# Retention into an ELU feed-forward layer on one core: an order written by hand replaced by steps that a planner lists, with FFN blocks of 256 tokens

## The chip, the cores and the metric

One NeuronCore of a Trainium2 chip runs the whole program in one launch. TensorE (PE in the profile, PEld for its weight loads) does the matrix products, VectorE (DVE) and ScalarE (ACT) the work that reads PSUM, GpSimd (POOL) works on SBUF only, and SyncE (SP) issues DMAs. DMAs issued by SP go through a hardware queue (q1 in the profile), those issued by GpSimd through a software queue (q0). The metric is the device time of the program in microseconds, as the median of its runs.

## The reference, cut to what matters

```python
# q, k, v: float32 (8, 8, 576, 64): batch, heads, sequence, head size
scores = (1 / sqrt(64)) * q @ k^T
gamma  = 1 - 2 ** (-5 - head)                       # one decay per head
D      = gamma ** (i - j) where i >= j, else 0
ret    = (scores * D) @ v
x      = ret laid out as (8 * 576 = 4608 tokens, 512)
h      = x @ w_in                                   # w_in (512, 2048)
g      = where(h > 0, h, exp(min(h, 0)) - 1)        # ELU
out    = g @ w_out                                  # w_out (2048, 512), out (4608, 512) float32
```

All inputs are float32. The decay factors into a power of gamma on q and one on k, so each kernel scales q and k while casting them to bf16 and needs only a 0/1 mask on the scores.

## The kernel before, in words

**Retention.** A batch of 576 positions is cut into five units: four main units (sequence half T of 256 positions, group w of four heads) and one tail of 64 positions with all eight heads. That makes 40 units. A unit is loaded by three DMAs of SP (`load`, L180; tails L174), scaled and cast (`cast`, L191: four 128x256 products for q and k, on POOL or DVE; L217 for v), and its q and k are transposed: the first nine units on PE through the identity (`turn_pe`, L241, with copies out of PSUM, L242), the others by a DMA transpose of SP (`turn`, L230). `stretch(u)` is one visit of PE to retention: it does the products with the carried state (`inter`) and with v (`values`) of unit u-1, the scores and the new state of unit u. Between them DVE masks the scores (L292, tails L286), adds up the state (L381, L383, L388) and POOL spreads it into block-diagonal form (L372). ACT copies the finished retention to `xt` in bf16 (L345, tails L334).

**FFN.** Tokens are worked in nine groups of 512. `ffn1(g, ft)` makes 128 rows of the hidden layer by four matmuls of 512 columns into one PSUM bank `ph`; ACT takes the exponential (`e`, L467), DVE subtracts one (`em`, L471) or ACT takes the ReLU in place (L469), and DVE joins both (`g`, L476 or L478). `ffn2(g, it, fts)` adds up 128 tokens of the output in the bank `pm` by sixteen matmuls of 512 columns; ACT copies it out (L488) and the store goes from POOL's queue (L491), for the last group from SP's. Group 1 is worked in two parts, of 320 and 192 tokens.

**Weights.** `load_w` (L151) loads w_in and w_out as 32 float32 tiles of 256 KB from SP, `cast_w` (L156) casts each to bf16, 31 of them on POOL and one on ACT.

**Order.** Every instruction is issued in an order written by hand (`pin` keeps program order on each engine). The loads of units 0 to 3 come first on SP, then the 32 weight tiles, then the loads of units 4 to 11. The retention of batch 0's main units is the start; then group 0's FFN; then group 1's with the stretches of the next units spread by hand between; and from group 2 on `run` spreads the stretches evenly between alternating FFN1 and FFN2 calls. A stretch is followed by the loads five units ahead, the casts three ahead and the transpose two ahead (`step`).

PSUM has eight banks: three for `ph` (also for PE transposes), one for `pm`, two for the scores, two for `x`. Almost all PE instructions are recorded at the helper's line L66.

Of the kernel before, what the change touches and what calls it, by code (L numbers as in the profile page):

```python
# [13 lines left out]
ALU = mybir.AluOpType  # L14


@with_exitstack
def kernel(
# [9 lines left out]
    nc = tc.nc  # L28
# [4 lines left out]
    NTOK = B * S  # L33
    P = 128
# [6 lines left out]
    TG = 512  # L41
    NTG = NTOK // TG
    MID = S // 2
    NS = B * NU
# [4 lines left out]
    raw = ctx.enter_context(tc.tile_pool(name="raw", bufs=10))  # L49
    nat = ctx.enter_context(tc.tile_pool(name="nat", bufs=4))  # L50
    tpool = ctx.enter_context(tc.tile_pool(name="tpool", bufs=4))
    ppool = ctx.enter_context(tc.tile_pool(name="ppool", bufs=2))
    rpool = ctx.enter_context(tc.tile_pool(name="rpool", bufs=4))
    xpool = ctx.enter_context(tc.tile_pool(name="xpool", bufs=3))
    gpool = ctx.enter_context(tc.tile_pool(name="gpool", bufs=2 * NFT + 2))
    epool = ctx.enter_context(tc.tile_pool(name="epool", bufs=4))
    opool = ctx.enter_context(tc.tile_pool(name="opool", bufs=4))

    ps_h = ctx.enter_context(tc.tile_pool(name="ps_h", bufs=3, space=PSUM))
    ps_m = ctx.enter_context(tc.tile_pool(name="ps_m", bufs=1, space=PSUM))  # L60
    ps_s = ctx.enter_context(tc.tile_pool(name="ps_s", bufs=1, space=PSUM))
    ps_x = ctx.enter_context(tc.tile_pool(name="ps_x", bufs=1, space=PSUM))

    pin = tc.keep_in_program_order
    def mm(*a, **kw):
        pin(nc.tensor.matmul(*a, **kw))  # L66
# [3 lines left out]


    ident = const.tile([P, P], BF16, name="ident")
    make_identity(nc, ident)
    zero = const.tile([P, 512], BF16, name="zero")
    nc.vector.memset(zero, 0.0)
# [33 lines left out]

    mask = const.tile([P, 2, 2, C], BF16, name="mask")  # L110
    nc.vector.memset(mask, 1.0)
    for c in range(2):
        for ek in range(2):
            for eq in range(2):
# [3 lines left out]
    mask_t = const.tile([ST, ST], BF16, name="mask_t")  # L118
    nc.vector.memset(mask_t, 1.0)
    nc.gpsimd.affine_select(out=mask_t, in_=mask_t, compare_op=ALU.is_ge, fill=0.0, base=0, pattern=[[1, ST]],  # L120
                            channel_multiplier=-1)


    s_mid = [const.tile([P, 2, P], BF16, name=f"s_mid{w}") for w in range(2)]
    s_end = [[const.tile([P, 2, P], BF16, name=f"s_end{w}{t}") for t in range(2)] for w in range(2)]
# [9 lines left out]
    engines = {"v": nc.vector.tensor_copy, "s": nc.scalar.copy, "p": nc.gpsimd.tensor_copy}  # L135
    staged = {}

    def weights(k):
        for i in (2 * k, 2 * k + 1):
            n, j = divmod(i, KJ)  # L140
            if n < KJ:
                c = slice(n * 512, (n + 1) * 512)
                yield i % 2, moe_w_in[j * P : (j + 1) * P, c], w_in_sb[:, j, c]
            else:
                f = i - KJ * KJ
                yield i % 2, moe_w_out[f * P : (f + 1) * P, :], w_out_sb[:, f, :]

    def load_w(k):
        staged[k] = raw.tile([P, 2, 4, 2, D], FP32, name="rqk", tag="rqk").rearrange("p i h e d -> p i (h e d)")
        for h, src, dst in weights(k):  # L150
            pin(nc.sync.dma_start(staged[k][:, h], src))  # L151

    def cast_w(k, eng="pp"):
        for h, src, dst in weights(k):
            if eng[h] != " ":
                pin(engines[eng[h]](dst, staged[k][:, h]))  # L156


    rawt, natt, trt, ptt, score_ps, total = {}, {}, {}, {}, {}, {}
    xps, begun = [None, None], set()  # L160

    def unit(u):
        b, r = divmod(u, NU)
        return b, r // 2, r % 2, r == FT

    def load(u, last=False):
        if u >= NS:
            return
        b, T, w, tail = unit(u)
        if tail:  # L170
            rqk = raw.tile([P, H, D], FP32, name="rqt", tag="rqt", bufs=2)
            rv = raw.tile([ST, H, D], FP32, name="rvt", tag="rvt", bufs=2)
            for dst, src in ((rqk[:ST], q), (rqk[ST:], k), (rv, v)):
                pin(nc.sync.dma_start(dst, src[b, :, FT * P :, :].rearrange("h p d -> p h d")))  # L174
        else:
            rqk = raw.tile([P, 2, 4, 2, D], FP32, name="rqk", tag="rqk")
            rv = raw.tile([P, 4, 2, D], FP32, name="rv", tag="rv", bufs=7)
            parts = [(rqk[:, 0], q), (rqk[:, 1], k), (rv, v)]
            for dst, src in parts[2:] + parts[:2] if last else parts:
                pin(nc.sync.dma_start(  # L180
                    dst.rearrange("p h e d -> p h (e d)"),
                    src[b, 4 * w : 4 * w + 4, 2 * P * T : 2 * P * (T + 1), :].rearrange("h (p e) d -> p h (e d)", e=2),
                ))
        rawt[u] = rqk, rv

    def cast_q(u, eng, i=0, es=(0, 1)):
        b, T, w, tail = unit(u)
        x = rawt[u][0][:, i].rearrange("p h e d -> p e h d")
        g = (gq, gk)[i][:, 2 * T : 2 * T + 2, 4 * w : 4 * w + 4].unsqueeze(3).to_broadcast([P, 2, 4, D])
        for e in es:  # L190
            pin(eng.tensor_tensor(natt[u][0][:, i, e], x[:, e], g[:, e], ALU.mult))  # L191

    def cast(u, q="p", v="p"):
        if u >= NS:
            return
        b, T, w, tail = unit(u)
        rqk, rv = rawt[u]
        if tail:
            qkn = nat.tile([P, H, D], BF16, name="qkt", tag="qkt", bufs=2)
            vn = nat.tile([ST, H, D], BF16, name="vt", tag="vt", bufs=2)  # L200
            g = gq[:, FT].unsqueeze(2).to_broadcast([P, H, D])
            for hs in (slice(0, H // 2), slice(H // 2, H)):
                pin(nc.gpsimd.tensor_tensor(qkn[:, hs], rqk[:, hs], g[:, hs], ALU.mult))
            pin(nc.gpsimd.tensor_copy(vn, rv))
        else:
            qkn = nat.tile([P, 2, 2, 4, D], BF16, name="qkn", tag="qkn")
            vn = nat.tile([P, 4, 2, D], BF16, name="vn", tag="vn", bufs=5)
            natt[u] = qkn, vn
            if q:
                cast_q(u, nc.vector if q == "v" else nc.gpsimd)  # L210
                cast_q(u, nc.gpsimd, 1)
            if v:
                cast_v(u, v)
        natt[u] = qkn, vn

    def cast_v(u, eng):
        pin(engines[eng](natt[u][1], rawt[u][1]))  # L217

    def turn_tile(u):
        n = 4 if unit(u)[3] else 8  # L220
        trt[u] = tpool.tile([P, n, P], BF16, name="qkT", tag=f"qkT{n}")
        return n

    def flat(u):
        return natt[u][0].rearrange("p h d -> p (h d)" if unit(u)[3] else "p i e h d -> p (i e h d)")

    def turn(u):
        if u < NS:
            turn_tile(u)
            pin(nc.sync.dma_start_transpose(trt[u], flat(u)))  # L230

    def turn_pe(u, eng="vs", between=0):
        n = turn_tile(u)
        for i in range(2):
            if i and between:
                warm(between)
            if i * 4 < n:
                p = ps_h.tile([P, 4, P], BF16, name="ptr", tag="ph")
                for j in range(4):
                    lo = (i * 4 + j) * P  # L240
                    pin(nc.tensor.transpose(p[:, j], flat(u)[:, lo : lo + P], ident))  # L241
                pin(engines[eng[i]](trt[u][:, i * 4 : i * 4 + 4], p))  # L242

    def queries(u, rows, hl, c):

        return trt[u].rearrange("p (i h) n -> p i h n", h=2)[rows, 0:2, hl, c * C : (c + 1) * C]
# [3 lines left out]

    def new_x():
        for c in range(2):
            xps[c] = ps_x.tile([P, 512], FP32, name="x", tag=f"x{c}")
        begun.clear()

    def acc_x(c, half, out, lhsT, rhs, to=None):

        first = not ({half} if half < 2 else {0, 1}) & {h for cc, h in begun if cc == (c, id(to))}
        begun.update(((c, id(to)), h) for h in ((half,) if half < 2 else (0, 1)))
        mm(out, lhsT, rhs, start=first, stop=True, skip_group_check=True)  # L260

    def scores(u):
        b, T, w, tail = unit(u)
        sc = ps_s.tile([P, 2, 512], FP32, name="sc", tag="sc")
        if tail:
            for hp in range(HP):
                for i in range(2):
                    r = slice(i * D, (i + 1) * D)
                    mm(sc[:ST, i, hp * ST : (hp + 1) * ST], trt[u][r, hp, ST:], trt[u][r, hp, :ST], start=True, stop=True)
        else:  # L270
            for hl in range(2):
                for ek in range(2):
                    for i in range(2):
                        r = slice(i * D, (i + 1) * D)
# [422 lines left out]
```

## Time and profile before

| | |
|---|---|
| time, median of 3 runs | 336.96 us (336.87 to 337.36) |
| span of the profiled execution | 333.9 us, 3.1 us under the median |
| PE busy | 303.7 us (91%) |
| DVE, ACT, POOL busy | 208.1, 178.8, 180.7 us (62%, 54%, 54%) |
| read and written in HBM | 36.70 and 9.44 MB |
| chain that ended last | PE 76%, POOL 9%, DVE 4%, DMA 3%, ACT 3% |

The profile is of one execution, so sums made from its rows are compared with its span, 333.9 us, and the 3.1 us around it are added to compare with a median. PE's busy time counts each matmul to its modelled end, so an isolated one counts for more than the pitch of a stream; a few matmul records are missing. In rows of the timeline a start time, a length and a count are given for instructions merged into one row.

### The profile page before, as it was taken

How to read it: one execution, taken by the hardware profiler on the slowest of the kernel's cores; microseconds unless marked ns; L12 is line 12 of the kernel's file. 1: busy time of each engine (PE TensorE's matmuls, PEld its weight loads, DVE VectorE, ACT ScalarE, POOL GpSimd, SP SyncE). 2: the span in 40 equal slices, each digit the busy share in tenths (PEclk: the TensorE clock that was granted, in tenths of full speed). 3: DMA queues.
4: the chain of work that ended last, by engine and by line, in shares of the span. 5: the costliest groups of instructions: out<-in, count | busy, mean ns of one | idle time of the engine just before them, and what ended most of it. 6: DMA issues, size and time to landing. Idle time of an engine off the chain costs nothing.

```text
span 333.9 us, 7841 instructions
## 1 busy us (share of the span) xinstructions
PE 303.7 (91%) x3049; PEld 154.4 (46%) x3092; DVE 208.1 (62%) x378; ACT 178.8 (54%) x364; POOL 180.7 (54%) x316
## 2 busy tenths in 40 slices
PE   7789985767679999999999999999999999999995
PEld 2443442444455554444545445444544544444342
DVE  3868626487747997666758666866677654454400
ACT  3666523555436766555565656555565556546411
POOL 5899564478979887442675666676574110000100
PEclk9999999999979999999999999999999999999999
DMA  7999999505999999854469957795421100000021
GB/s 213 312 339 375 287 320 274 153 2 145 222 267 216 254 244 219 176 159 143 110 127 207 243 123 174 181 232 112 96 63 49 64 33 31 33 31 32 33 94 63
DMA packets 100293, 53.86 MB, mean 161 GB/s; under 512 B 44448, under 2 KB 93600, under 8 KB 100256
## 3 DMA queue, kind: packets, MB, share of 16 engines
q1 hardware_dynamic: 97696, 44.97, 56.5%
q0 software_dynamic: 2560, 8.39, 8.4%
q8 instruction: 24, 0.39, 0.5%
q14 instruction: 13, 0.11, 0.1%
HBM read 36.70 MB, written 9.44 MB: 138 GB/s over the span
## 4 chain that ended last, share of the span: by engine, by line
PE 76%; POOL 9%; DVE 4%; DMA 3%; ACT 3%; issue 2%; SPq 0%; POOLq 0%; ACTq 0%; DVEq 0%
PE pm L66 35%; PE ph L66 32%; PE x L66 5%; PE sc L66 3%; POOL qkn L191 3%; POOL w_in_sb L156 3%; DMA qkT<-qkn 2%; DMA rqk<-in_q_dram 2%; DVE pt L292 1%; DVE g L478 1%; ACT ot L488 1%; DVE em L471 1%; POOL s_mid_147 L372 1%; ACT xt L345 1%; ACT ph L469 1%
## 5 line engine op out<-in xcount | busy, mean ns | idle before, releaser
L66 PE MATMUL ph<-xt,w_in_sb 128*128 128x512 bf16 (+2 forms) x611 | 145.7, 358 | 6.6 <-DVE g L478 3.7
L66 PE MATMUL pm<-w_out_sb,g 128*128 128x512 bf16 x564 | 144.1, 380 | 3.2 <-ACT ot L488 1.7
L467 ACT ACTIVATE e<-ph 128x512 f32<-128x512 f32 (+2 forms) x152 | 87.3, 575 | 90.0 <-PE ph L66 78.8
L66 PEld LDWEIGHTS <-w_in_sb 128*128 128x128 bf16 x640 | 59.3, 98 | 66.2 <-issue 8.0
L66 PEld LDWEIGHTS <-g 128*128 128x128 bf16 x576 | 55.7, 98 | 70.1 <-issue 7.9
L476 DVE SCALAR_TENSOR_TENSOR g<-e,ph 128x512 bf16<-128x512 f32 (+2 forms) x80 | 50.3, 633 | 48.1 <-ACT ph L469 45.4
L471 DVE TENSOR_SCALAR em<-e 128x512 bf16<-128x512 f32 (+2 forms) x76 | 43.2, 569 | 31.4 <-ACT e L467 31.4
L491 POOL DMA_DIRECT2D out_dram<-ot x32 | 18.4, 576 | 77.4 <-ACT ot L488 77.4
L478 DVE SCALAR_TENSOR_TENSOR g<-ph,em 128x512 bf16<-128x512 f32 (+2 forms) x80 | 50.7, 638 | 3.7 <-DVE em L471 0.5
L469 ACT ACTIVATE ph<-ph 128x512 f32<-128x512 f32 (+2 forms) x76 | 43.3, 570 | 0.0
L292 DVE TENSOR_TENSOR pt<-sc,mask 128x1024 bf16<-128x1024 f32 x31 | 37.8, 1218 | 7.2 <-PE sc L66 7.2
L191 POOL TENSOR_TENSOR qkn<-rqk,gk 128x256 bf16<-128x256 f32 x64 | 38.5, 621 | 3.5 <-DMA rqk<-in_k_dram 3.5
L345 ACT CAST xt<-x 128x256 bf16<-128x256 f32 (+1 forms) x70 | 23.7, 419 | 26.3 <-PE x L66 26.2
L488 ACT COPY ot<-pm 128x512 f32<-128x512 f32 x36 | 21.1, 589 | 20.1 <-PE pm L66 20.1
L191 POOL TENSOR_TENSOR qkn<-rqk,gq 128x256 bf16<-128x256 f32 x52 | 31.5, 625 | 0.1
L372 POOL TENSOR_TENSOR s_mid_147<-mid,diag 128x256 bf16<-128x256 f32 x16 | 9.9, 618 | 26.8 <-DVE mid L383 14.2
L372 POOL TENSOR_TENSOR s_mid_146<-mid,diag 128x256 bf16<-128x256 f32 x16 | 9.7, 606 | 26.2 <-DVE mid L383 20.0
L66 PE MATMUL sc<-qkT 64*64 64x128 bf16 (+1 forms) x576 | 16.1, 222 | 3.2 <-DMA qkT<-qkn 2.8
L217 POOL CAST vn<-rv 128x512 bf16<-128x512 f32 x28 | 18.8, 671 | 0.0
L66 PEld LDWEIGHTS <-qkT 64*64 64x64 bf16 x576 | 10.0, 107 | 8.8 <-DMA qkT<-qkn 3.1
L66 PE MATMUL x<-pt,vn 64*64 64x128 bf16 x496 | 13.1, 221 | 0.0
L241 PE MATMUL ptr<-ident,qkn 128*128 128x128 bf16 x64 | 7.3, 227 | 5.7 <-POOL qkn L191 2.3
(79 smaller groups left out, 184.0 us busy)
## 6 DMA issues: line engine op xcount, KB each, us to landing
rqk<-in_q_dram SPq DMA_DIRECT2D x32, 256.0 KB, 4.5
rqk<-in_k_dram SPq DMA_DIRECT2D x32, 256.0 KB, 5.0
rv<-in_v_dram SPq DMA_DIRECT2D x32, 256.0 KB, 5.3
out_dram<-ot POOLq DMA_DIRECT2D x32, 256.0 KB, 3.8
rqk<-in_moe_w_in_dram SPq DMA_DIRECT2D x16, 256.0 KB, 5.7
rqk<-in_moe_w_out_dram SPq DMA_DIRECT2D x16, 256.0 KB, 5.5
rqt<-in_q_dram SPq DMA_DIRECT2D x8, 128.0 KB, 4.2
rqt<-in_k_dram SPq DMA_DIRECT2D x8, 128.0 KB, 4.1
```

What stands on the lines that cost most here:

```text
L66: pin(nc.tensor.matmul(*a, **kw))
L191: pin(eng.tensor_tensor(natt[u][0][:, i, e], x[:, e], g[:, e], ALU.mult))
L217: pin(engines[eng](natt[u][1], rawt[u][1]))
L292: pin(nc.vector.tensor_tensor(pt.rearrange("p i h n -> p (i h) n"), sc.rearrange("p i (h n) -> p (i h) n", h=2), mask.rearrange("p k e r - ...
L345: pin(engines[eng[c]](dst, src[:, :, :, a // 2 : (a + n) // 2]))
L372: pin(eng.tensor_tensor(dst.rearrange("p h (j d) -> p h j d", j=2), src.unsqueeze(2).to_broadcast([P, 2, 2, D]), diag.unsqueeze(1).unsquee ...
L467: pin(nc.scalar.activation(e[:, :m], ph[:, :m], AF.Exp))
L469: pin(nc.scalar.activation(ph[:, :m], ph[:, :m], AF.Relu))
L471: pin(nc.vector.tensor_scalar_add(em[:, :m], e[:, :m], -1.0))
L476: pin(nc.vector.scalar_tensor_tensor(dst, e[:, c], -1.0, ph[:, c], ALU.add, ALU.min))
L478: pin(nc.vector.scalar_tensor_tensor(dst, ph[:, c], 0.0, em[:, c], ALU.max, ALU.min))
L488: pin(nc.scalar.copy(ot, pm))
```

## The change

The program is no longer issued in the order in which it is written. Each step (a load, a cast, a transpose, a stretch, an FFN piece, a store) is added to a list with the engines that may do it, a cost on each, what it depends on, a rank, and the buffer slots that it takes. A planner in the kernel then goes through time: it takes of the steps that are ready the one that can start first, of those that start within 0.05 us on the same engine the one of lowest rank, and gives it the engine on which it would end first. It does so eight times, with the transfers' times taken from the round before, keeps the order with the earliest end, and issues the program in that order. Beside this:

- FFN blocks have 256 tokens: two per batch (`seq` 0 to 15), and two blocks "A" and "B" of four tails each. A PSUM bank holds two 128-row pieces of the hidden layer side by side.
- A block needs two main units. Batch by batch the units are 0 to 3, 4 to 7, then the tails of both batches as one item, and so on: 36 items.
- Weights are cast by the DMA itself: eight transfers from POOL's queue, each reading 1 MB, each listed after a given step of the first units.
- The middle step of the ELU may go to ACT, DVE or POOL, the copies out of PSUM to ACT or DVE, the casts of q and k to POOL or DVE.
- All single `ph`, `pm`, transpose and early state banks share four PSUM slots "f"; scores have one slot of two banks, `x` one of two.
- Items 0 to 7 are transposed on PE, the others by DMA.

```diff
+HOP = {"PE": 0.24, "DVE": 0.08, "ACT": 0.08, "POOL": 0.1}
+LANES = 8
...
+            picks = list(best.values())
+            first = min(picks, key=lambda c: (c[1], c[2]))
+            same = [c for c in picks if c[3] == first[3] and c[1] <= first[1] + 0.05]
+            _, s, _, eng, pay, op = min(same, key=lambda c: (c[2], c[1]))
...
+def W_GATE(items, n):
+    return [items[2].cq[1, 1], items[3].cq[1, 1], items[3].bm, items[3].be][n]
+def WO_GATE(items, n):
+    return items[4].cq[1, 1] if n < 2 else items[5].cq[1, 1]
+LEAD = 64
+SLOTS = {
+    "f": 4, "sc": 1, "x": 1,
+    "rqk": 8, "rv": 8, "qkn": 5, "vn": 6, "qkT": 5, "pt": 3,
+    "rqt": 4, "rvt": 2, "qkt": 4, "vt": 2, "qkTt": 4, "ptt": 2,
+    "xt": 5, "g": 20, "e": 4, "em": 4, "ot": 4, "mid": 4, "end": 4, "s_mid": 4, "s_end": 8,
+}
...
-    def load_w(k):
-        staged[k] = raw.tile([P, 2, 4, 2, D], FP32, name="rqk", tag="rqk").rearrange("p i h e d -> p i (h e d)")
-        for h, src, dst in weights(k):
-            pin(nc.sync.dma_start(staged[k][:, h], src))
-    def cast_w(k, eng="pp"):
-        for h, src, dst in weights(k):
-            if eng[h] != " ":
-                pin(engines[eng[h]](dst, staged[k][:, h]))
...
+    seq = list(range(2 * B))
+    seq = [*seq[:B], "A", *seq[B:], "B"]
...
+    for it in items:
+        it.rank = it.n * 4 - 64 if it.early else place[it.blk] * 16 - LEAD + 6 * (it.half if it.tail else it.w)
...
+    def load_w_in(n0, n1, after):
+        c = slice(n0 * 512, n1 * 512)
+        def emit(op):
+            pin(nc.gpsimd.dma_start(w_in_sb[:, :, c], moe_w_in[:, c].rearrange("(j p) n -> p j n", p=P)))
+        op = add(f"wi{n0}", {"POOL": 1.1}, [], emit, -1000, dma=2.8 * (n1 - n0), after=after)
+    def load_w_out(n, after):
+        def emit(op):
+            pin(nc.gpsimd.dma_start(w_out_sb[:, 4 * n : 4 * n + 4],
+                                    moe_w_out[n * 512 : (n + 1) * 512, :].rearrange("(f p) n -> p f n", p=P)))
+        w_out_ld[n] = add(f"wo{n}", {"POOL": 1.1}, [], emit, -1000, dma=2.8, after=after)
...
+    def ffn1(blk, p):
...
+        rank = i * 16 + 2 * p
...
+            for f in range(2):
+                ft = 2 * p + f
+                for j in range(KJ):
+                    mm(ph[:, f * TB : (f + 1) * TB], w_in_sb[:, j, ft * P : (ft + 1) * P], xt[:, j],
+                       start=(j == 0), stop=(j == KJ - 1))
...
+        f1 = add(f"F1_{blk}_{p}", {"PE": 0.873}, [*xdone[blk], w_in_ld[p // 2]], emit, rank,
+                 take=[T("f", hkey, [P, 512], FP32)], use=[("xt", blk)], after=chain.get(1))
...
+        md = add(f"md_{blk}_{p}", {"ACT": 0.55, "DVE": 0.5, "POOL": (0.75, 0.1)}, [ex], emit_m, rank,
...
+    def ffn2(blk, it, c, per, rank):
...
+            for ft in range(c * per, (c + 1) * per):
+                g = tiles["g", blk, ft // 2].rearrange("p (f n) -> p f n", f=2)
+                mm(pm, g[:, ft % 2, it * P : (it + 1) * P], w_out_sb[:, ft], start=(ft == 0), stop=(ft == NFT - 1))
...
+    for n in range(4):
+        load_w_in(n, n + 1, W_GATE(items, n))
...
+    for n in range(4):
+        load_w_out(n, WO_GATE(items, n))
+    for i, blk in enumerate(seq):
+        for p in range(NP):
+            ffn1(blk, p)
+        if i == 0:
+            for c in range(8):
+                for it in range(2):
+                    ffn2(blk, it, c, 2, (i + 1) * 16 + 1 + 2 * c)
+        else:
+            for it in range(2):
+                for c in range(4):
+                    ffn2(blk, it, c, 4, (i + 1) * 16 + 8 * it + 2 * c + 1)
+    order = plan.run({"PE": 1.3, "DVE": 2.2, "ACT": 3.0, "POOL": 4.4, "SP": 0.8})
...
+        if op.eng == "PE":
+            if op.name.startswith("iv"):
+                for _ in range(int((op.start - last - 0.3) / 0.25)):
+                    mm(tiles[op.take[0][1]][:, 0], zero[:, :P], zero, start=True, stop=True)
```

## The prediction

> **What bounds the kernel now.** I read the page first (TensorE, "PE", is busy 91% of the span and holds 76% of the chain that ended last), then the busy time by stretch, to see where the other 9% lies.
>
> ```profile
> core 0: us, PE busy (x) PEld busy (x) DVE busy (x) ACT busy (x) POOL busy (x), PEclk, DMA share, GB/s
> 20.00:30.00 10.00, 8.90 (x38) 3.61 (x38) 7.98 (x14) 7.11 (x14) 10.00 (x18) 1.00 0.97 338
> 50.00:60.00 10.00, 5.95 (x126) 3.15 (x117) 5.22 (x9) 3.58 (x8) 4.96 (x8) 1.00 1.17 276
> 60.00:70.00 10.00, 6.48 (x76) 4.27 (x75) 7.11 (x17) 5.59 (x14) 4.00 (x8) 1.00 0.29 82
> 80.00:90.00 10.00, 7.56 (x146) 5.40 (x146) 7.57 (x17) 3.91 (x9) 10.00 (x18) 1.00 0.80 175
> 90.00:110.00 20.00, 16.18 (x239) 10.09 (x242) 11.76 (x26) 9.32 (x21) 17.29 (x30) 0.91 1.25 243
> 110.00:130.00 20.00, 19.79 (x253) 10.35 (x255) 18.22 (x30) 14.49 (x31) 17.54 (x30) 1.00 1.23 233
> 200.00:230.00 30.00, 29.74 (x337) 15.13 (x341) 20.93 (x34) 17.53 (x36) 19.02 (x32) 1.00 0.78 183
> ```
>
> From 110 us on PE is 99% busy: nothing but less PE work helps there. Before 110 us it has holes, and GpSimd (POOL) is full at 20 to 30 and at 80 to 90 us. The chain of waits, in order of time, names what the holes wait for:
>
> ```profile
> 18.33 4.10 POOL w_in_sb L156 x7
> 23.58 5.04 POOL w_in_sb L156 x8
> ...
> 77.94 2.36 POOL qkn L191 x4
> 80.99 2.29 POOL qkn L191 x4
> 83.83 1.55 POOL qkn L191 x3
> 87.29 6.14 DMA qkT<-qkn
> ```
>
> POOL casts the weights until 39 us, only then the inputs of the later batches, and PE runs out of FFN work while it waits for them and for the transposes behind them. The PE timeline gives the prices of PE work:
>
> ```profile
> 84.03 0.83 PE L66 MATMUL ph<-xt,w_in_sb 128*128 128x192 bf16 x8
> 84.92 0.81 PE L66 MATMUL pm<-w_out_sb,g 128*128 128x512 bf16 x3
> 85.57 0.82 PE L66 MATMUL ph<-xt,w_in_sb 128*128 128x192 bf16 x8
> ...
> 115.52 0.28 PE L66 MATMUL x<-qkT,s_mid_147 128*128 128x128 bf16 x2
> 115.73 0.42 PE L66 MATMUL sc<-qkT 64*64 64x128 bf16 x16
> 115.97 0.39 PE L66 MATMUL x<-pt,vn 64*64 64x128 bf16 x16
> 116.20 0.29 PE L66 MATMUL x<-vn,qkn 64*64 64x64 bf16 x16
> 116.42 1.90 PE L66 MATMUL ph<-xt,w_in_sb 128*128 128x512 bf16 x7
> ```
>
> Groups of four 512-wide matmuls follow each other at 0.864 us in the chain, so 0.216 us each. The fourth pm record of 84.92 is missing (it began at 85.57 - 0.864 = 84.70), so eight 192-wide matmuls, each with its own weight load, took 0.67 us: 84 ns each, where 192/512 of 216 is 81. A retention stretch costs PE 0.79 to 1.01 us in the timeline from 110 to 137 us (here 116.42 - 115.52 = 0.90); I take 0.88.
>
> **The ledger of before**, against its span of 333.9 us. First FFN matmul at 19.6. FFN: 576 + 576 matmuls of 512 columns (the 320- and 192-wide ones counted as one) x 0.216 = 248.8. Retention behind that: 36 units x 0.88 = 31.7, and ten groups of four PE transposes of 0.25 = 2.5, together 34.2. The end, from the last matmul at 330.0 over a copy of 0.59 and a store: 3.9. Sum 306.5; the remaining 27.4 us is lost on PE between 20 and 110 us, a 3.4 us half-clock spell at 90 to 94 us included (the granted clock of 0.91). The median of the runs, 336.96, is 3.1 above the span.
>
> **The change part by part.**
>
> *FFN blocks of 256 tokens.* FFN1 becomes 1152 matmuls of 256 columns. By the two rows the excess over pure width is about 3 ns per matmul, so 106.7 + 2.8 = 109.5 ns: 126.1 us instead of 124.4. FFN2 stays at 576 x 0.216 = 124.4. Sum 250.5, +1.7. Weight loads (98 ns mean, 128 columns) stay under the 109 ns, as they did even under 84. ACT and DVE get the same number of 128x512 instructions (144 of each step); the middle one may go to POOL, where the nearest row, the 128x512 cast, is 0.64 us; POOL has over 10 of 30 us free from 200 us on.
>
> *Block 0 needs two units, not four.* Retention for it could be done at about 14 us, so the first FFN matmul waits for weights instead.
>
> *Weights by eight casting transfers of 1 MB from POOL's queue.* Gone: 31 POOL casts x 0.65 = 20 us, and SP's 32 loads that stood ahead of the next units' loads. New: eight issues on POOL, each 0.58 (the store's row, 128 rows of 2 KB) to four times that, 2.3 (512 rows): 4.6 to 18.4 us of POOL over 30 us; I take 1.2 each, nearer to the store. Behind an issue stand POOL's casts of units 3 to 5, which PE does not need until block 1. The first is listed after unit 2's second k cast, which ended at 12.6 (11.23 + 1.34) in before. Transfer: no row casts while it moves. One end is the 338 GB/s row, 3.1 us per MB; the other is the software queue's store, 256 KB in 3.8 us from issue to landing, 15 us per MB if nothing overlapped. By the packet times q0 moved 8.39 MB in 8.4% of 16 engines' span, 18.7 GB/s per engine, 3.5 us per MB on 16. Units 3 to 5 share the engines; I take 4.0 per chunk. First chunk: 12.6 + 1.2 + 1.2 (the 2.0 us of the last 256 KB stores less 0.8 of moving) + 4.0 = 19.0. The fourth: 31.0, and FFN1 of block 0 ends 1.75 later at 32.8. In these 13.8 us PE has 7.0 of FFN1 and some 3 of retention: 3.8 lost.
>
> The page "DMA: Bandwidth & Descriptors" of the Trainium skill (section "Anatomy of one DMA") fits a software-queue transfer as 2.0 us plus bytes at 436 GB/s; by it a lone 1 MB takes 4.4 us end to end, and no run here yet shows one. A rule speaks against the change: "SBUF — State Buffer" (summary of rules) says that descriptor generation on GpSimd starves while VectorE is in its two-port modes, and advises the hardware queue. The 32 stores of before, beside a DVE at 62%, took 542 to 731 ns, median 582, so this trace shows little of it; had each issue its worst spread (+0.15 us), eight would add 1.2 us.
>
> *W_out.* Chunks land at 4.0 spacing: 35, 39, 43, 47 us. From 32.8 to 47 PE has FFN1 of blocks 1 and 2 (14.0) and three quarters of block 0's FFN2 (5.2): covered, if units 4 and 5 are through by 40 us. Their loads now stand ahead of all later ones, and POOL's five casts (3.1 us a unit) start once unit 3's are done, some 15 us earlier than the 44 us of before. Were that cover gone, up to 7 us would be lost here.
>
> *Units ahead of need.* The planner ranks retention four blocks ahead. A block is 13.9 us of FFN plus 2 stretches; its two units cost POOL 2 x (5 x 0.63 + 2 x 0.65) = 9 us. So the waits at 60 to 97 us should go. In-order queues stay: a late transfer holds PE, and a store listed on POOL holds the casts behind it, but four blocks of lead cover that. I keep 1.0 us for it; bounds 0 and 18 (1 us per block, see rivals).
>
> *Tails in pairs.* A tail adds about 0.43 to its stretch (scores 0.12, inter 0.21, values 0.10), 3.4 for eight; four double ones do the same work: 3 to 4. Zero.
>
> *End.* Same copy and store, one more issue on SP (0.35): 4.2.
>
> **Sum.** 19.0 + 3.8 + 250.5 + 34.2 + 1.0 + 4.2 = 312.7 us of span, 21.2 less; plus 3.1: **315.8**. At 3.1 us per chunk, with retention at the lower end and nothing lost later, it is 310; with unit 2's k cast shared between DVE and POOL and all chunks up to 3 us earlier, 306.
>
> **Rivals.**
> (1) *Slow casting transfers, slower than before.* Place: POOL's software queue, 15 to 47 us. Once g's 20 buffers (2.5 blocks, 17.5 us) and three quarters of one FFN2 (5.2) are used up, PE waits for the last w_out chunk at 15 + 8x. Then remain 250.5 - 22.7 + 26.2 + 5.2 = 259.2, so the span is 274.2 + 8x. It beats my sum above x = 4.8 us per MB and before above 7.5 us (140 GB/s). At 15 us: 394 of span, 397 in time. For it: no cast transfer in the trace. Against: 3.5 us per MB by packets.
> (2) *A listed order that does not fit.* PE is in order; if each of 18 blocks waits 1 us for PSUM, for ACT or for a store that holds POOL, 18 us go back: 334, still faster; from 1.2 us per block on, slower. Against: ACT and DVE have a third of each stretch free after 110 us, and before loses only 0.6 us of 208 there with as few PSUM banks.
> (3) *Weight loads uncovered by narrow matmuls:* 1152 x 98 ns = 113 us more, 429. The 192-wide row excludes nearly all of it (0.67, not 1.46 us).
> (4) *PE fills no better early:* the later units stay late for another reason and only the start and FFN1's 1.7 us differ: 337.
>
> **How the numbers follow.** The forecast's mechanism (306 to 322) 0.70. Rivals on the faster side, x between 5 and 7.5 or up to 1.1 us per block (322 to 336): 0.16. Rival 4, within 0.2% (0.7 us, about what a measurement of this kernel can tell from no change): 0.02. Rivals 1 and 2 beyond their break-even, and 3: 0.12. Faster 0.86, same 0.02, slower 0.12. The range runs from 305 to 331 (x = 6.7, or 0.8 us per block), leaving out 2 in 10.
>
> **What would show it.** Right: no POOL cast to w_in_sb or w_out_sb, eight software transfers with some 4 us spacing, first ph matmul at 18 to 20 us, 256-wide groups of eight at 0.87 to 0.88 us, PE 99% busy from about 35 us on, no half clock at 90 us. Wrong: ph matmuls that wait for w_in_sb or w_out_sb past 47 us (rival 1), PE idle behind DVE g or ACT ot in most blocks (rival 2), eight 256-wide matmuls in over 1 us (rival 3).

## The result, and the profile after

The change makes the kernel slower: **355.06 us** as the median (350.9 to 356.7) against 336.94 of before, a ratio of 1.0488 with a 95% interval of 1.0423 to 1.0554. The forecast of 315.8, and its range up to 331, were wrong, and so was the sign. The profiled execution took 355.25 us, with a span of 353.5, where the sum had 312.7. One of the four runs, 356.7, fell in a slower state that some executions of a program show; without it the median is 354.9.

The busy time by stretch shows where it is. (Columns: stretch, its length, then busy time and instructions of PE, PEld, DVE, ACT, POOL; granted PE clock, DMA share, GB/s.)

```profile
10.00:20.00 10.00, 8.44 (x122) 4.43 (x121) 6.87 (x13) 2.08 (x5) 6.55 (x10) 0.50 1.19 289
20.00:30.00 10.00, 4.30 (x48) 2.29 (x47) 3.06 (x4) 2.32 (x5) 9.98 (x16) 0.50 1.16 200
30.00:40.00 10.00, 0.00 (x0) 0.00 (x0) 0.00 (x0) 0.00 (x0) 0.91 (x2) 0.50 1.21 201
...
60.00:70.00 10.00, 1.69 (x7) 0.77 (x7) 3.10 (x6) 4.62 (x11) 1.28 (x3) 0.50 1.22 234
...
110.00:118.00 8.00, 5.06 (x108) 3.86 (x93) 7.86 (x7) 4.50 (x12) 7.26 (x13) 0.95 0.72 177
118.00:345.00 227.00, 226.62 (x2653) 156.94 (x2651) 163.48 (x286) 119.23 (x227) 89.77 (x152) 0.99 0.48 103
```

From 118 us on PE is full, as the forecast had it from 35 us on. The loss lies before that, and in a form that no rival described: from 30 to 40 us PE, DVE and ACT do nothing at all, and POOL next to nothing, while the DMA engines are busy throughout. Nothing is short of an engine; everything waits for something in flight. The table of waits names it (engine, line, what ended the wait: us in total, times, longest):

```profile
ACT vt L490 <- DMA rvt<-in_v_dram: 29.1, 2, 16.5
PE sc L220 <- DVE qkT L426: 14.8, 2, 14.5
ACT vn L408 <- DMA rv<-in_v_dram: 14.7, 5, 5.0
POOL qkt L471 <- DMA rqt<-in_k_dram: 12.0, 2, 7.7
PE f L220 <- DVE g L793: 11.6, 2, 11.4
```

The timelines of ACT, DVE and PE, side by side, show how one load held everything (start, length, instruction, and in brackets the idle time before it and what ended it):

```profile
40.61 0.62 ACT L490 CAST vt<-rvt 128x512 bf16<-128x512 f32 x1 [16.53 <-DMA rvt<-in_v_dram]
41.14 0.43 ACT L673 CAST xt<-x 128x256 bf16<-128x256 f32 x1
41.44 0.58 ACT L426 COPY qkT<-f 128x512 bf16<-128x512 bf16 x1
...
65.27 0.62 ACT L490 CAST vt<-rvt 128x512 bf16<-128x512 f32 x1 [12.54 <-DMA rvt<-in_v_dram]
```
```profile
41.60 0.45 DVE L673 CAST xt<-x 128x256 bf16<-128x256 f32 x1 [18.54 <-ACT xt L673]
41.95 0.41 DVE L426 COPY qkT<-f 128x512 bf16<-128x512 bf16 x1
```
```profile
42.41 0.64 PE L220 MATMUL sc<-qkT 64*64 64x128 bf16 x16 [14.45 <-DVE qkT L426]
42.99 1.89 PE L220 MATMUL f<-xt,w_in_sb 128*128 128x256 bf16 x8
```

ACT stands from 24.1 to 40.6 us in front of one cast: the v of item 8, the first pair of tails, which block "A" needs, the ninth block of the FFN. Behind that cast in ACT's queue is an `xt` copy; DVE's `xt` waits for it, and behind that in DVE's queue is the `qkT` copy that PE's next scores (of item 3) need. PE therefore reaches the first FFN matmul, listed behind these scores, at 43.0 us. At 52.7 us ACT stops again, for the v of item 17. PE's granted clock was 0.50 from 8.0 to 45.5 and again from 59.2 to 72.8 us.

Why were these casts listed there? The planner's own times for this order, beside what the chip did (us; "landed" is when the load's data were there):

```
load                         planned to land   landed
v of item 7                       10.6          22.9
v of item 8, first of two loads   12.8          37.2
v of item 10                      13.8          47.8
v of item 17, first of two        19.2          64.3
```

In the planner every load lands 2.9 us after its issue, however many others are in flight. So it believes that the loads of 18 items are there by 20 us, and lists each cast on whichever engine is free that early. Of its eight rounds the first has this assumption; the later ones take each transfer's delay from the round before, which had a different order. The ends that it planned were 307.9, 849.5, 311.4, 637.7, 313.2, 498.0, 313.2 and 449.3 us; it kept the earliest, the first round's.

### The profile page after: what moved, and what is told of

It is laid out like the page before. It is cut to its first block, busy times and chain, and to the rows that moved or that the text cites. A ratio compares the mean times of both kernels' runs of the same rounds, so it can differ in the third digit from the quotient of the medians.

```text
span 353.5 us, 8928 instructions
## 1 busy us (share of the span) xinstructions
PE 308.3 (87%) x3601; PEld 208.5 (59%) x3601; DVE 226.1 (64%) x401; ACT 164.3 (46%) x317; POOL 152.1 (43%) x267
## 4 chain that ended last, share of the span: by engine, by line
PE 77%; DMA 8%; DVE 5%; SPq 5%; ACT 2%; POOL 1%; issue 1%; DVEq 0%; ACTq 0%
PE f L220 68%; DMA rvt<-in_v_dram 6%; PE x L220 4%; PE sc L220 3%; SPq L335 3%; DVE em L785 3%; DMA rv<-in_v_dram 2%; SPq L350 1%; DVE g L795 1%; SPq L358 1%; ACT e L773 1%; DVE pt L638 1%; PE f L420 1%; POOL qkn L392 1%; POOL s_mid L612 0%
## 5 line engine op out<-in xcount | busy, mean ns | idle before, releaser
L220 PE MATMUL f<-w_out_sb,g 128*128 128x512 bf16 x576 | 145.5, 381 | 11.6 <-DVE g L793 11.6
L220 PE MATMUL f<-xt,w_in_sb 128*128 128x256 bf16 x1152 | 150.2, 276 | 4.1 <-DVE g L795 4.0
L220 PEld LDWEIGHTS <-w_in_sb 128*128 128x128 bf16 x1152 | 111.8, 99 | 41.4 <-issue 5.1
L773 ACT ACTIVATE e<-f 128x512 f32<-128x512 f32 x144 | 86.0, 597 | 95.6 <-PE f L220 88.1
L785 DVE TENSOR_SCALAR em<-e 128x512 bf16<-128x512 f32 x108 | 58.8, 545 | 45.7 <-ACT e L773 45.3
L795 DVE SCALAR_TENSOR_TENSOR g<-f,em 128x512 bf16<-128x512 f32 x108 | 74.4, 690 | 9.8
L392 POOL TENSOR_TENSOR qkn<-rqk,gq 128x256 bf16<-128x256 f32 x56 | 34.2, 624 | 14.2 <-PE x L220 11.2
L612 POOL TENSOR_TENSOR s_mid<-mid,diag 128x256 bf16<-128x256 f32 x31 | 19.2, 618 | 47.1 <-ACT mid L595 38.1
L638 DVE TENSOR_TENSOR pt<-sc,mask 128x1024 bf16<-128x1024 f32 x32 | 38.9, 1216 | 0.6 <-PE sc L220 0.3
L793 DVE SCALAR_TENSOR_TENSOR g<-e,f 128x512 bf16<-128x512 f32 x36 | 24.5, 682 | 15.5 <-ACT f L783 15.0
L827 ACT COPY ot<-f 128x512 f32<-128x512 f32 x36 | 21.1, 587 | 17.5 <-PE f L220 17.5
L220 PE MATMUL sc<-qkT 64*64 64x128 bf16 x512 | 14.5, 236 | 15.5 <-DVE qkT L426 14.8
L783 ACT ACTIVATE f<-f 128x512 f32<-128x512 f32 x36 | 21.6, 600 | 0.0
L612 POOL TENSOR_TENSOR s_end<-end,diag 128x256 bf16<-128x256 f32 x30 | 18.8, 626 | 3.3 <-DVE end L604 3.1
## 6 DMA issues: line engine op xcount, KB each, us to landing
w_out_sb<-in_moe_w_out_dram POOLq DMA_DIRECT2D x4, 512.0 KB, 18.8
```

The costliest lines, as they stand in the source:

```text
L392: pin(alu[op.eng].tensor_tensor(tiles[key][:, i, e], tiles[raw][:, :, e], g, ALU.mult))
L612: pin(alu[op.eng].tensor_tensor(tiles[key].rearrange("p h (j d) -> p h j d", j=2), tiles[src].unsqueeze(2).to_broadcast([P, 2, 2, D]), dia ...
L638: pin(nc.vector.tensor_tensor(tiles["pt", n].rearrange("p i h n -> p (i h) n"), tiles["sc", n].rearrange("p i (h n) -> p (i h) n", h=2), m ...
L773: pin(nc.scalar.activation(tiles[ekey], tiles[hkey], AF.Exp))
L783: pin(nc.scalar.activation(ph, ph, AF.Relu))
L785: pin(alu[op.eng].tensor_scalar_add(em, e, -1.0))
```

## The experiments

Ratios are to the runs of before on the same chip.

**1. Two tail casts later.** Only the v casts of items 8 and 17 (`cv8`, `cv17`) are moved in the list, to where PE needs them, with the later loads that take their buffers.

```diff
+    for use, moved in (("S8", ("cv8", "ldt2026", "ldt2126")), ("S18", ("cv17", "ldt2035", "ldt2135"))):
+        late = [op for op in order if op.name in moved]
+        order = [op for op in order if op.name not in moved]
+        i = [op.name for op in order].index(use)
+        order[i:i] = late
```

> The planner's order is kept but for two casts on ACT (vt of the first two tail items) and the four rvt loads that need their buffers, which are listed just ahead of the stretch that uses the cast. Theory A (ACT, in order, stands 16.5 and 12.5 us behind two loads that the order takes for landed): first FFN matmul at 27 to 30 us instead of 43 us (first w_in chunk landed at 26.8), no gap of 11 us at 56 us; the next v casts on ACT still wait for loads that landed at 44 to 53 us, so 328 to 340 us in all. Theory B (the transfers themselves are late, whoever waits): 348 to 357 us, with PE waiting for w_in_sb or w_out_sb where it waited for ACT.

Measured: 345.51 us, ratio 1.0269 (1.0219 to 1.0319). The first FFN matmul came at 27.4 us instead of 43.0, as theory A has it, so these casts were what held it. The time missed A's range, and B's too. But the next casts on ACT take their place:

```profile
ACT vn L408 <- DMA rv<-in_v_dram: 27.2, 6, 15.1
```

Of 15.6 us gained at the start 9.5 stay. The two casts are a symptom; the order has more of them.

**2. Not the first round.** The planner may keep any round but the first; it kept one that it planned at 311.4.

```diff
-            if best is None or end < best[0]:
+            if turn and (best is None or end < best[0]):
```

> The planner may not keep the order of its first round, in which every load lands 2.0 us plus its own length after its issue whatever else is in flight; all else as in the change. Theory A (the fault is an order made with landing times of idle queues): the tail casts are listed at 40 and 65 us, ACT has no wait of over 5 us for a load, 316 to 332 us. Theory B (the queues are simply too full until 50 us): at least 345 us.

Measured: 345.80 us, 1.0246 (1.0200 to 1.0292). First FFN matmul at 22.9, and ACT waits at most 3.3 us for a load, as theory A has it; but PE is still idle elsewhere, the longest 5.86 us for a transpose of a tail, `qkTt`, at 90 to 96 us, and the time lies in theory B's range. Either the queues are simply too full, or a landing time taken from another order is no better than a constant; this run does not tell, experiment 8 does.

**3. The kernel before with the casting transfers alone.** Its order by hand stays; the 32 loads and 32 casts go.

```diff
-    cast_w(0, "s ")
+    load_cast(0)
...
-    cast_w(0, " p")
+    load_cast(1)
...
-    for kk in range(6, 16):
-        load_w(kk)
-        cast_w(kk)
+    for n in range(4, 8):
+        load_cast(n)
```

> The kernel before, with its order by hand, and only the weights changed: eight casting transfers of 1 MB on POOL's queue where the first weight casts stood, no weight loads on SP, no casts. If casting transfers are good in themselves (3.6 us per MB in the trace of the change, 20 us of POOL casts gone, later units' loads 8 to 10 us earlier): 318 to 333 us. If their landing behind each other costs as much as the POOL casts did: 334 to 340 us. If they are what made the change slower: above 342 us.

Measured: 348.57 us, 1.0348 (1.0296 to 1.0399), 11.6 us slower. POOL lost 13 us of work (180.7 to 167.4), yet the first FFN matmul is at 26.0 and waits for w_in, and later for w_out, 10.1 us together, where PE in the kernel before waits 0.3 us for weights. SP's queue is held too: each row is one load held at issue while the chunks move.

```profile
PE ph L66 <- DMA w_in_sb<-in_moe_w_in_dram: 6.0, 1, 6.0
PE pm L66 <- DMA w_out_sb<-in_moe_w_out_dram: 4.1, 1, 4.1
```
```profile
34.50 3.50 SPq L173 DMA_DIRECT2D rqt<-in_q_dram  x1
38.05 3.49 SPq L173 DMA_DIRECT2D rqt<-in_k_dram  x1
41.59 3.49 SPq L173 DMA_DIRECT2D rvt<-in_v_dram  x1
```

The 1 MB chunks land 3.4 to 3.7 us apart, and in the same time only one load of SP gets through. So the forecast's price per chunk was near the mark; but the first chunk landed 9.5 us after its issue, where the forecast had 6.4, and what the chunks take from the loads beside them was not priced at all. How much of the 11.6 us comes from the held loads is not separated here; the two waits for weights come close to it.

**4. The w_in transfers first on POOL's queue**, ahead of the v cast that held them in the changed kernel.

```diff
+    moved = ("wi0", "wi1", "wi2", "wi3")
+    early_w = [op for op in order if op.name in moved]
+    order = [op for op in order if op.name not in moved]
+    i = [op.name for op in order].index("cv3")
+    order[i:i] = early_w
```

> The planner's order is kept, but the four w_in transfers are issued some 6 us earlier, ahead of the cast of unit 3's v on POOL. Theory A (ACT's wait for the tail's v load sets the first FFN matmul): that load still lands at 36 to 41 us, first FFN matmul at 40 to 45 us, 350 to 357 us. Theory B (late weights set it): first FFN matmul at 33 to 37 us, 340 to 348 us.

Measured: 351.01 us, 1.0408 (1.0365 to 1.0452). The first chunk now landed at 20.7 us and the others 3.6 to 3.7 behind each other, very near the forecast's 19.0 and 4.0. The time lies in theory A's range, but the first FFN matmul came at 51.4, later than before the edit and than A's 40 to 45:

```profile
ACT vn L408 <- DMA rv<-in_v_dram: 25.8, 5, 10.8
PE x L220 <- ACT xt L673: 14.2, 1, 14.2
```

From 20.7 us on (26.8 in the changed kernel) it is not w_in that holds PE. The earlier chunks make the loads of v later (that of item 7 landed at 36.7 instead of 22.9), and the casts listed for them hold ACT.

**5. Units behind the weights**, on experiment 3: the loads of units 4 to 11 leave from POOL's queue, behind the chunks.

```diff
-                pin(nc.sync.dma_start(
+                pin((nc.gpsimd if FT <= u <= FT + 7 else nc.sync).dma_start(
```

> The kernel before with the eight casting transfers (as in e3), and the loads of units 4 to 11 issued from POOL's queue behind them, so that nothing shares the engines with the weights. Theory C (the engines are full at some 350 GB/s until 50 us, and what costs is the order in which bytes land: in e3 the later units' loads on SP stood ahead of and beside the weights): weight chunks 2.7 to 3.0 us apart instead of 3.6, the last w_out chunk at 38 to 43 us instead of 51, 326 to 340 us. Theory D (casting transfers cost that much in themselves): 345 to 352 us, as e3.

Measured: 355.32 us, 1.0521 (1.0476 to 1.0567): outside both ranges. The edit brought a wait of its own. First FFN matmul at 21.8, but POOL's timeline has its issues waiting for earlier transfers, one by one, until 42 us; they go on until 58 us, with its casts behind them. Two rows of it, and the stretch in which PE runs dry:

```profile
33.49 0.75 POOL L179 DMA_DIRECT2D rqk<-in_k_dram  x1 [2.11 <-DMA w_out_sb<-in_moe_w_out_dram]
35.98 0.75 POOL L179 DMA_DIRECT2D rv<-in_v_dram  x1 [1.74 <-DMA w_out_sb<-in_moe_w_out_dram]
```
```profile
50.00:60.00 10.00, 0.23 (x2) 0.13 (x2) 0.00 (x0) 0.00 (x0) 7.23 (x11) 0.63 1.02 249
```

One sign of theory C is there: with no load of SP beside them the chunks landed 2.5 to 3.4 us apart, the last at 41.3. Whether loads behind the chunks are better in themselves is not decided by it.

**6. Items in one line with the weights, in the planner**, on experiment 2: the loads of items 4 to 8 leave from POOL's queue too, in a fixed order with the chunks, and loads have fewer buffers to run ahead in.

```diff
-    "rqk": 8, "rv": 8, "qkn": 5, "vn": 6, "qkT": 5, "pt": 3,
-    "rqt": 4, "rvt": 2, "qkt": 4, "vt": 2, "qkTt": 4, "ptt": 2,
+    "rqk": 8, "rv": 4, "qkn": 5, "vn": 6, "qkT": 5, "pt": 3,
+    "rqt": 2, "rvt": 1, "qkt": 4, "vt": 2, "qkTt": 4, "ptt": 2,
...
+    line = [w_in_ld[n] for n in range(4)] + [items[n].ld[c] for n in (4, 5) for c in "qkv"] + \
+        [w_out_ld[n] for n in range(4)] + [items[n].ld[c] for n in (6, 7) for c in "qkv"] + \
+        [items[8].ld[c] for c in ((0, 0), (1, 0), (0, 1), (1, 1), ("v", 0), ("v", 1))]
+    for one, two in zip(line, line[1:]):
+        two.after = one
```

> e2 with the loads of items 4, 5, 6, 7 and of the first tail item issued from POOL's queue in one line with the weights (w_in, items 4 and 5, w_out, items 6 and 7, tail), and fewer buffers for v and tail loads (rv 4, rqt 2, rvt 1), so that no load of SP runs ahead of the weights. Theory C: chunks 2.7 to 3.0 us apart, w_in landed by 26 us, PE busy in over 85% of 30 to 100 us, 318 to 335 us. Theory D: 340 to 350 us.

Measured: 345.89 us, 1.0247 (1.0199 to 1.0295), the same as experiment 2 and in theory D's range, not in C's. The first FFN matmul moved to 18.3; PE then waits 13.1 us for a `qkTt` instead.

**7. Weights by SP, as before**, on experiment 2: 32 loads of SP and 32 casts as planned steps. Left of the change: the planner, 256-token blocks, pairs of tails.

```diff
-            pin(nc.gpsimd.dma_start(w_in_sb[:, :, c], moe_w_in[:, c].rearrange("(j p) n -> p j n", p=P)))
+            pin(nc.sync.dma_start(tiles[key], src))
...
+        done.append(add(f"cw{m}", {"POOL": 0.65, "ACT": (0.62, 0.3), "DVE": (0.5, 0.5)}, [ld], emit, m - 45, use=[key]))
```

> e2 with the weights loaded as in before: 32 float32 tiles of 256 KB by SP, listed between the loads of items 3 and 4, and cast by POOL, ACT or DVE as the planner likes; planner, blocks of 256 and tail pairs stay. Theories C and D both: w_in cast by 27 to 32 us, w_out by 40 to 44 us, 316 to 332 us. Theory E (orders listed ahead of time do not hold on the chip, whatever the transfers): 338 to 350 us.

Measured: 348.13 us, 1.0311 (1.0283 to 1.0339), in theory E's range. With no casting transfer at all the kernel is as slow as experiment 2, so these transfers are not the main cause. Its longest wait on PE:

```profile
100.86 0.26 PE L220 MATMUL sc<-qkTt 64*64 64x64 bf16 x1 [11.83 <-DMA qkTt<-qkt]
```

That transpose was planned to land at 67.9 us and landed at 100.8.

**8, 9, 10. Landing times that belong to the order.** If the orders are bad because their landing times are, only those have to be changed. All loads and transposes of a plan go over one line, one after the other; one round, no times from another order. The same edit in three kernels: the change itself (8), experiment 7 (9), experiment 6 (10). The order that the change kept was its first round's too, so between it and 8 the landing rule is all that differs.

```diff
-    def run(self, began, rounds=8):
+    def run(self, began, rounds=1):
...
-                op.done = s + late.get(op.name, 2.0 + op.dma)
+                wire = max(wire, s + 1.3) + op.dma
+                op.done = wire + 0.6
```

> The change with one thing altered in the planner: a transfer's landing is worked out while the order is made, with one line of all transfers behind each other (it begins 1.3 us after its issue or when the one before has ended, takes its own length, lands 0.6 us later), in one round; nothing else. The planner's end is then 315 us. Theory F (the orders kept so far rest on landing times that belong to no such order, and the chip, in order on every engine, waits where a load comes later than listed): no wait of ACT for a load over 5 us, the landing of each load within 6 us of the plan up to 100 us, 318 to 330 us in all. Theory E (lists made ahead of time do not hold on the chip in any case): 338 to 350 us.

> e7 (planner, weights by SP as float32 and cast on the engines) with the landing times of e8; the planner's end is 322 us. Theory F: 324 to 336 us, against 348 of e7. Theory E: 338 to 350 us.

> e6 (casting transfers, items 4 to 8 in one line with them on POOL's queue) with the landing times of e8; the planner's end is 318 us. Theory F: 320 to 333 us, against 346 of e6. Theory E: 338 to 350 us.

Measured:

```
                                          from      to       ratio to before
8  on the change                         355.06   335.89   0.9933 (0.9899 to 0.9967)
9  on 7, weights by SP                   348.13   323.96   0.9589 (0.9545 to 0.9632)
10 on 6, items in line with the weights  345.89   328.86   0.9761 (0.9707 to 0.9815)
```

The same few lines are worth 19, 24 and 17 us. Kernel 8 fell short of the expected 318 to 330 (its loads are up to 19 us late, and ACT still waits up to 6.5 us for one) and landed between the two theories' ranges; 10 lies in its range, and 9 at the lower edge of it. Number 9 beats both kernels of this case. PE's busy time in the first 120 us, read with its granted clock (the third column from the end), tells the four apart, in the order before, after, 8, 9 (the line is that of the stretch from 0 to 120 us in each trace):

```profile
0.00:120.00 120.00, 96.16 (x1226) 53.43 (x1243) 79.32 (x168) 62.13 (x135) 89.84 (x166) 0.99 0.96 243
```
```profile
0.00:120.00 120.00, 79.79 (x943) 51.45 (x944) 64.50 (x120) 44.37 (x89) 62.69 (x116) 0.78 1.06 221
```
```profile
0.00:120.00 120.00, 97.28 (x1293) 65.32 (x1293) 78.57 (x147) 52.59 (x106) 75.65 (x139) 0.87 0.97 209
```
```profile
0.00:120.00 120.00, 106.92 (x1500) 72.45 (x1500) 81.28 (x161) 64.37 (x129) 99.66 (x181) 0.94 1.08 268
```

And the plan now says what happens (us, planned to land and landed):

```
                             7               8               9
                        plan   chip     plan   chip     plan   chip
v of item 7             41.1   49.9     29.9   48.7     53.1   50.1
v of item 8             42.9   52.7     48.4   51.1     57.6   52.7
transpose of item 8     67.9  100.8     56.4   57.1     69.3   65.2
v of item 17            54.4   73.4     89.0  101.8     97.2   94.2
```

In 9 plan and chip stay within 6 us of each other. In 8 the transposes keep to the plan within 3 us up to 66 us, but the v of item 7 is 19 us late: the planner knows one line, and the chip gives a load of SP about one turn per 1 MB chunk. With the same landing rule, kernel 8 with the casting transfers is 12 us slower than kernel 9 without, and kernel 10 is 5 us slower, though the planner put both ahead of 9 (315.1 and 318.4 against 321.7). (Under the rule of experiment 2 it was the other way, 345.8 with and 348.1 without; there the order's own faults are larger.)

**11. A truer price for the weight tiles.** Experiment 9 with 0.68 us for a tile, where they landed 0.65 to 0.70 apart, in place of 0.9.

```diff
-take=[T("rw", key, [P, 512], FP32)], dma=0.9)
+take=[T("rw", key, [P, 512], FP32)], dma=0.68)
```

> e9_one_wire_sp with one constant changed: the planner takes 0.68 us for a weight tile of 256 KB (the trace of e9 has them landing 0.65 to 0.70 us apart) instead of 0.9. Planned end 311.6 instead of 321.7. Theory F (an order is worth as much as its landing times are true): the plan now follows the chip more closely in the first 60 us, the first FFN matmul comes 2 to 5 us earlier than 18.6 or its successors wait less, and the time falls to 314 to 322. Rival I (what is left of e9's 324 is the chip's own drift from the plan, in costs of instructions and not of loads): 321 to 328, same as e9.

Measured: 327.2 us (322.8 to 329.3), 0.9724 (0.9666 to 0.9782), in rival I's range. The four runs are 322.8, 325.7, 328.7 and 329.3; the lower two lie with the 322.2 to 324.6 of experiment 9, so whether the kernel is any slower than 9 is not shown. What is shown is that a plan 10 us shorter, 311.6, brought nothing. The v of item 7 was planned at 46.1 and landed at 49.7, the transpose of item 12 at 76.5 and 82.5: late, by up to 9.5 us before 120 us, where experiment 9's came up to 6 us early. So the plan's times are no truer than 9's, only off to the other side, and how exact they have to be stays open.

**12. `em` never on DVE**, on experiment 8 (the last section says why).

```diff
-        md = add(f"md_{blk}_{p}", {"ACT": 0.55, "DVE": 0.5, "POOL": (0.75, 0.1)}, [ex], emit_m, rank,
+        md = add(f"md_{blk}_{p}", {"ACT": 0.55, "POOL": (0.75, 0.1)}, [ex], emit_m, rank,
```

> e8_one_wire with the step that makes em taken off VectorE: the planner may put it on ScalarE or GpSimd alone (it puts 143 of 144 on ScalarE; planned end 317.0 instead of 315.1). In e8 one such instruction on VectorE took 5.93 us and one 3.90, where the median is 0.43, each beside a row of back to back GpSimd instructions. Theory L (these long instructions hold the FFN back by what they are too long): no VectorE instruction over 1.5 us is left, and the time falls by 3 to 9 us to 327 to 333. Rival M (they fall beside other waits, the late loads of v above all): 334 to 341, or more where ScalarE, with some 60 us more to do, becomes late. Rival N: VectorE's other instructions are blocked as long when GpSimd runs on; then long ones stay in the trace, under another line.

Measured: 336.27 us, 0.9971 (0.9945 to 0.9998), where experiment 8 had 335.89: rival M's range. No DVE instruction over 1.3 us is left, and PE is busy for all of 80 to 100 us where 8 had 16.89 us; but PE did 2.7 us less in the first 60 us (37.7 against 40.4) and 1.8 less from 140 to 300. Taking the long instructions away gained nothing. Since the edit also moves work to ACT (busy 204.2 us instead of 156.0) and makes another order, it does not price them by themselves.

## Why the prediction was wrong

*First FFN matmul at 19.0: it came at 43.0.* This step failed, with 24.0 of the 40.8 us between 312.7 and 353.5. The first chunk's transfer is a small part of it: it was issued at 18.8 instead of 12.6, because two v casts listed on POOL ahead of it waited for their loads (2.55 and 0.62 us) and other casts stood between, and landed at 26.8, 8.0 after issue where the sum had 6.4. The other 16 us are PE waiting for DVE, DVE for ACT, and ACT for a load. The sentence that failed is "Retention for it could be done at about 14 us": the last `xt` copy of block 0 ended at 23.6, because ACT stood 4.99 and 1.77 us in front of the v casts of items 5 and 6, and PE, in its listed order, then stood in front of the scores of item 3. I read the 14 us off the units' work and did not ask in which order their neighbours' loads and casts would be listed, on which engine, and against what landing time.

*3.8 and 1.0 us lost behind that: by the same ledger it was 353.5 - (43.0 + 250.5 + 34.2 + 4.6) = 21.2.* From 50 to 118 us PE's idle time in the rows by ten is 16.7 us, 12.6 of it from 50 to 70; most of the rest is work at half clock, from 43.0 to 45.5 and from 67.6 to 72.8 us: by an estimate half of the 7.0 us that PE is busy in them, 3.5. The sentence "a late transfer holds PE, and a store listed on POOL holds the casts behind it, but four blocks of lead cover that" failed. The lead of four blocks is a rank, and a rank only decides between steps that could start within 0.05 us of each other; it protects nothing from a step that is listed too early.

*Rival 2 was the right one, with the wrong place.* It looked for a microsecond per block on PSUM, ACT or stores, all along. There the kernel is full: 226.62 of 227 us. The misfit sits in the first 118 us, on loads.

*Rival 1's price was nearly what I took: the chunks landed 3.3 to 4.2 us apart, where I had 4.0,* and its break-even of 4.8 was not reached. PE waited for w_out nowhere after the change. What it lacked is the other side of sharing: a first chunk that lands 8.0 to 9.5 us after its issue, and one load of SP per chunk. Put into the kernel before, the transfers cost 11.6 us. In the changed kernel itself, exchanging these transfers for loads of SP gained only once the plan's times were mended.

*Right:* the FFN. Groups of four and eight follow each other as forecast, 184.13 - 182.39 = 1.74 us for the pair, and 144 pairs make 250.6 (250.5):

```profile
182.39 1.04 PE L220 MATMUL f<-xt,w_in_sb 128*128 128x256 bf16 x8
183.26 1.03 PE L220 MATMUL f<-w_out_sb,g 128*128 128x512 bf16 x4
184.13 1.04 PE L220 MATMUL f<-xt,w_in_sb 128*128 128x256 bf16 x8
```

The end is 4.6 (4.2). Around the span lie 1.75 us in this execution, not 3.1. No POOL cast of weights is left, and POOL is free enough: kernel 9 shows that the mechanism (full PE, units ahead of need) does exist, at 324 us, with the weights loaded by SP and cast on the engines. It stays 8 us above the forecast; where these go was not followed up.

*The page "SBUF — State Buffer"* was weighed for its rule that descriptor generation starves. The chunk issues took 0.75 to 0.95 us, so nothing of it was seen, but DVE stood idle during six of the eight, which makes this a weak test; my 1.2 was too much.

## What to carry to other kernels

An order listed ahead for in-order engines can be spoiled by the landing times that it was listed with, here by 17 to 24 us: before believing a planned end, compare the landing times of its loads with what the queue delivered in a trace, above all when many loads are listed closer together than they can move. A step listed early costs nothing only if it cannot wait; a cast for a far item, put in front of near work on ACT, held PE for 14.5 us. And a big transfer on a second queue is priced twice, once for itself and once for the loads that share the engines with it.

## What the runs showed of the hardware that I had not expected

**A DVE instruction that stands for several microseconds.** `em`, 128x512 from SBUF to SBUF, takes 0.43 us. In kernel 8 one took 3.90 and one 5.93, and the latter ended only when POOL came to the end of a row of instructions that followed each other without a gap. DVE, then POOL:

```profile
77.59 5.93 DVE L786 TENSOR_SCALAR em<-e 128x512 bf16<-128x512 f32 x1 [0.52 <-ACT e L774]
83.62 0.69 DVE L796 SCALAR_TENSOR_TENSOR g<-f,em 128x512 bf16<-128x512 f32 x1
```
```profile
77.53 1.19 POOL L393 TENSOR_TENSOR qkn<-rqk,gq 128x256 bf16<-128x256 f32 x2
78.67 1.18 POOL L393 TENSOR_TENSOR qkn<-rqk,gk 128x256 bf16<-128x256 f32 x2
79.79 0.60 POOL L409 CAST vn<-rv 128x512 bf16<-128x512 f32 x1
80.36 1.17 POOL L393 TENSOR_TENSOR qkn<-rqk,gq 128x256 bf16<-128x256 f32 x2
81.50 1.17 POOL L393 TENSOR_TENSOR qkn<-rqk,gk 128x256 bf16<-128x256 f32 x2
82.63 0.60 POOL L409 CAST vn<-rv 128x512 bf16<-128x512 f32 x1
```

The changed kernel has two such (3.49 and 4.30 us), experiment 10 two (6.07 and 2.54), the kernel before none above 0.9. The four in the changed kernel and in kernel 8 ended within 0.5 us of the end of such a row, the two of experiment 10 inside one. The Trainium skill, "SBUF — State Buffer", section "Who interferes with whom", says that DVE in a two-port mode and GpSimd share a port pair as an exclusive lock, held for the whole instruction, and that the other blocks fully. That fits, if `em` runs in such a mode, which no run here shows; but here DVE stood beside ten instructions in a row, not one. Of the 33 `em` of kernel 8 that ran wholly beside a busy POOL, 11 took no more than 0.46 us, so what starts it stays open.

**One load per chunk.** While casting transfers of 1 MB move (some 3.6 us each), SP's queue gets one load of 256 KB through per chunk, a fifth of the bytes read: in kernel 8 five in a row landed at 31.0, 34.7, 38.9, 42.5 and 46.2 us. In kernel 9, without casting transfers, such loads land one per 0.9 us, and the weight tiles of 256 KB landed 0.65 to 0.70 us apart. The chunks pay too: with no load of SP beside them (experiment 5) they landed 2.5 to 3.4 us apart.
